# Eleven result tiles, stores behind the loads, and three smaller moves in a scheduled attention-and-MoE kernel

## The chip, the cores and the metric

One core of one Trainium2 chip. The metric is the device time of one execution in microseconds (us); where several runs are given, their median. Engines are named as in the profile: PE (matmul), DVE (VectorE), ACT (ScalarE), POOL (GpSimd), SP (which issues DMAs). Each engine works through its own instructions in order and waits on semaphores for the others.

## The reference

```
kv  = einsum('bhsd,bhse->bhde', k, v)        # 8 batches, 8 heads, 576 positions, 64 wide
out = einsum('bhsd,bhde->bhse', q, kv)
out = out / sqrt(mean(out*out, -1) + 1e-6) * g_norm
x   = out, heads side by side, as [4608, 512]

h   = x @ w_in                               # [4608, 1024]
e   = exp(h - max(h));  sm = e / (sum(e) + 1e-9)
u   = h * sm
ln  = (u - mean(u)) / sqrt(var(u) + 1e-6) * g_ln
y   = ln @ w_out                             # [4608, 512]
```

The kernel takes exp(h) without the maximum and doesn't divide by the sum: u = h e^h, and the missing factor goes into the variance's small constant. The mean and g_ln are folded into w_out ahead of time (w_mean, w_center), so that the last matmul's rows only need one factor each, rstd.

## The kernel before

**Tiling.** The 4608 tokens are nine chunks of 512. Chunks 0 to 7 are eight ninths of the batches 0 to 7; chunk 8 is the last ninth of all of them (q_last, collected by the pieces ql0 to ql7). Head pairs share 128 partitions.

**Pieces.** Nothing is looped in the order that it runs. Each piece of work has a name, is registered with `plan.add` (its engine, what it needs, the tiles it takes and uses) and is called in the order of one text, ORDER (lines 68 to 121). That text was written by a planner; the kernel only reads it. A token like `b1.0/dve@ob4` is: piece b of chunk 1, part 0, on DVE, its result in the slot ob4. Slots are single buffers: L (9 KB a partition; k and v of a batch, u, squares), M (4.6 KB; q, e, x), ob (results), osq, lss, rst (small ones) in SBUF, and P (two banks) and S (one bank) in PSUM. A slot is reused as soon as its last user is done; semaphores for that are set by the framework from the order. SLOTS (line 19) gives the counts for the planner.

**One chunk** runs through these pieces:

- k, v, q: loads, cast to bf16 by GpSimd's DMA queue (line 269; "a" and "b" are halves in batches 0 and 1). wi and wo load the weights.
- kv: k^T v of a batch on PE, 4 head pairs, into a P slot; kc.0, kc.1, kc.2: three copies out of it into kvd (line 319). Part 0 is the matrix as it lies, parts 1 and 2 are its two halves with the partitions turned over, for heads whose q lies in the other half.
- qt, qc: q turned by PE and copied out (chunks 0 to 4); qx: q turned by a DMA on SP (chunks 5 to 8).
- o: q times kv on PE; sq, s, ln, ex (ScalarE and PE; the mean square over a head by a matmul, then its root); x on DVE scales o into the input of the MoE part. Chunks 6 to 8 have rows instead of features up: o, sq, vd, vl, vg, x, xt, where vg is a product on GpSimd and xt a DMA transpose on SP.
- h: x times w_in on PE; e: exp on ScalarE; u: h times e on DVE; r: squares of u, for the variance. For chunks 0 to 2 (features up) r is a full tile of squares, g adds up pairs of e on GpSimd, z sums u, r and g over the features by matmuls, y and st turn that into the variance. For chunks 3 to 8 (rows up) e, u and r give their sums by the way (accum_out), st joins the three (row_stats, line 710) and t turns u by a DMA on SP.
- rs: the root of the variance on ScalarE; a: u times w_out on PE into a P or S slot; b: its rows scaled by rstd, on DVE or ScalarE, into an ob slot; d: the store, from SP's, GpSimd's or (chunk 8) ScalarE's queue. Chunk 8's last part goes in two halves of columns, a8.3|0 and a8.3|1.

**The gate.** `gate` (line 341) is a small copy on GpSimd that reads the last q loaded, q7, and stands ahead of the first DMA transpose, t3.0: no transpose starts before the loads are done. warm0 to warm8 are matmuls on zeros between the first pieces.

**Lines of the steps below.** 206 warm, 269 loads, 314 kv, 173 and 175 copies (kc, qc, ql, casts), 343 gate, 359 qt, 407 and 470 o, 420 sq, 435 s, 439 ln, 443 ex, 453 x, 495 vg, 572 and 581 h, 592 and 599 e, 607 and 612 u, 622 and 624 r of chunks 0 to 2 (ScalarE, GpSimd), 630 and 632 r of chunks 3 to 8 (ScalarE, DVE), 637 t, 643 g, 691 z, 714 to 720 row statistics, 767 and 774 a, 782 and 784 b, 799 and 801 d.

Of the kernel before, what the change touches and what calls it, by code (L numbers as in the profile page):

```python
# [857 lines left out]
```

## Time and profile before

| | |
|---|---|
| median of 3 runs | 182.4 us (181.66 to 182.57) |
| profiled execution | 181.77 us, span 179.7 us |
| granted PE clock | 0.999 |
| read from memory, written | 32.54 MB, 9.44 MB |

The profile shows one execution. A row of the timeline gives start, length (us), engine, line, operation, result and operands, how often, and in brackets the idle time ahead of it and what ended that. A row of groups gives line, engine, operation, shapes and count, then busy time and mean length (ns), then the idle time ahead and who ended it. A row of DMA issues gives the queue, the count, the size of each and the median time to landing. The table of windows gives, for each stretch, its length, the busy time (and instructions) of PE, weight loads, DVE, ACT and POOL, the granted clock, the DMA engines' mean share and GB/s. The chain of waits gives start, length and what the end was waiting for.

### The profile page before, as it was taken

Reading aid. Unit: us, or ns where it says so; the run is one execution under the profiler, and the core shown is the slowest. Engines: PE = TensorE matmul, PEld = TensorE weight load, DVE = VectorE, ACT = ScalarE, POOL = GpSimd, SP = SyncE. Lnnn points to the kernel's source line nnn. Section 1 sums busy time; section 2 is a strip of 40 time slices with the busy share of each in tenths; the row PEclk is TensorE's granted clock in tenths of the full one; section 3 lists DMA queues with packets and bytes.
Section 4 is the critical chain, followed back from the end, with each engine's and each line's share of the span. In section 5 each row is a group of like instructions: output and inputs, shape, how many; then the busy total and the mean of one; then the engine's idle time right before and its main releaser. Section 6 shows DMA issues by size and latency. Waiting matters only on the chain.

```text
span 179.7 us, 4520 instructions
## 1 busy us (share of the span) xinstructions
PE 164.9 (92%) x1808; PEld 81.1 (45%) x1831; DVE 127.1 (71%) x222; ACT 128.1 (71%) x239; POOL 71.9 (40%) x83
## 2 busy tenths in 40 slices
PE   6899958699999999999998999899999999999990
PEld 3344435345435565454443444444445444444450
DVE  2327599258874776667998869999788987948630
ACT  2377794593899687979879898469979746986210
POOL 7941596040899998100140006501132960222000
PEclk9999999999999999999999999999999999999999
DMA  5999999999999999999799999999998689968994
GB/s 170 252 207 275 353 208 209 205 208 222 248 233 232 209 207 198 277 214 206 157 172 203 206 216 220 152 256 245 171 227 239 99 166 248 200 139 215 175 256 125
DMA packets 60424, 37.81 MB, mean 210 GB/s; under 512 B 42140, under 2 KB 55204, under 8 KB 60404
## 3 DMA queue, kind: packets, MB, share of 16 engines
q0 software_dynamic: 15456, 20.16, 58.1%
q1 hardware_dynamic: 44036, 15.87, 44.1%
q10 hardware_dynamic: 912, 1.51, 3.1%
q8 instruction: 14, 0.23, 0.5%
q14 instruction: 6, 0.05, 0.1%
HBM read 32.54 MB, written 9.44 MB: 234 GB/s over the span
## 4 chain that ended last, share of the span: by engine, by line
PE 63%; DMA 22%; DVE 6%; issue 3%; POOL 1%; SPq 1%; ACT 1%; POOLq 0%; DVEq 0%; ACTq 0%
PE ps_S L767 20%; PE ps_P L581 19%; DMA sb_M<-in_q_dram 9%; PE ps_P L572 8%; PE ps_P L767 5%; DMA out_dram<-sb_ob 4%; DMA sb_L<-in_v_dram 4%; DMA sb_M<-sb_M 3%; PE ps_S L359 2%; DVE sb_ob L784 2%; PE ps_P L314 2%; PE ps_P L407 2%; DMA sb_L<-sb_L 2%; PE ps_P L691 1%; PE ps_S L435 1%
## 5 line engine op out<-in xcount | busy, mean ns | idle before, releaser
L767 PE MATMUL ps_S<-w_out_sb,sb_L 128*128 128x512 bf16 x220 | 53.1, 379 | 2.9 <-issue 2.4
L581 PE MATMUL ps_P<-w_in_sb,sb_M 128*128 128x512 bf16 x188 | 42.7, 379 | 1.0 <-ACT kvd L173 0.8
L767 PEld LDWEIGHTS <-sb_L 128*128 128x128 bf16 x280 | 26.4, 98 | 33.4 <-issue 3.3
L612 DVE SCALAR_TENSOR_TENSOR sb_L<-ps_P,sb_M 128x1024 bf16<-128x1024 f32 x24 | 29.1, 1222 | 8.4 <-ACT sb_M L599 8.2
L599 ACT ACTIVATE sb_M<-ps_P 128x1024 f32<-128x1024 f32 x24 | 24.5, 1023 | 8.2 <-PE ps_P L581 7.1
L581 PEld LDWEIGHTS <-sb_M 128*128 128x128 bf16 x192 | 18.7, 98 | 23.3 <-issue 0.9
L495 POOL TENSOR_TENSOR sb_M<-rr,g_rep 128x1024 f32<-128x1024 f32 x6 | 12.3, 2061 | 30.4 <-ACT rr L491 23.7
L572 PE MATMUL ps_P<-sb_M,w_in_sb 128*128 128x512 bf16 x94 | 21.9, 379 | 0.1
L607 DVE TENSOR_TENSOR sb_L<-ps_P,sb_M 128x1024 bf16<-128x1024 f32 x12 | 14.6, 1222 | 8.2 <-ACT sb_M L592 8.2
L453 DVE SCALAR_TENSOR_TENSOR sb_M<-ps_P,g_cols,sb_rst 128x512 bf16<-128x512 f32 x24 | 18.0, 790 | 2.9 <-ACT sb_rst L443 2.6
L784 DVE TENSOR_SCALAR sb_ob<-ps_S,rstd 128x512 f32<-128x512 f32 (+1 forms) x19 | 13.8, 735 | 7.7 <-PE ps_S L767 2.2
L592 ACT ACTIVATE sb_M<-ps_P 128x1024 f32<-128x1024 f32 x12 | 12.2, 1024 | 6.9 <-PE ps_P L572 6.9
L643 POOL TENSOR_TENSOR sb_M<-sb_M 128x512 bf16<-128x512 f32 x12 | 15.1, 1278 | 4.9 <-ACT sb_M L592 4.8
L420 ACT ACTIVATE sb_osq<-ps_P 128x512 bf16<-128x512 f32 x24 | 13.4, 596 | 4.6 <-PE ps_P L407 4.6
L630 ACT ACTIVATE sb_M<-sb_L 128x1024 bf16<-128x1024 bf16 x14 | 14.6, 1047 | 0.0
L572 PEld LDWEIGHTS <-w_in_sb 128*128 128x128 bf16 x96 | 9.2, 98 | 10.5 <-issue 0.2
L801 POOL DMA_DIRECT2D out_dram<-sb_ob x10 | 6.3, 633 | 16.4 <-DVE sb_ob L784 8.8
L632 DVE SCALAR_TENSOR_TENSOR sb_M<-sb_L 128x1024 bf16<-128x1024 bf16 x10 | 12.8, 1276 | 0.1
L443 ACT ACTIVATE sb_rst<-sb_lss 128x512 f32<-128x512 f32 x20 | 12.0, 632 | 0.1
L767 PE MATMUL ps_P<-w_out_sb,sb_L 128*128 128x512 bf16 x47 | 11.4, 379 | 0.1
L206 PE MATMUL ps_S<-zeros 128*128 128x512 bf16 (+1 forms) x18 | 8.5, 591 | 1.8 <-DVE zeros L188 1.5
L624 POOL TENSOR_TENSOR sb_L<-sb_L 128x1024 bf16<-128x1024 bf16 x4 | 7.6, 1910 | 6.1 <-DVE sb_L L607 6.0
(96 smaller groups left out, 211.2 us busy)
## 6 DMA issues: line engine op xcount, KB each, us to landing
out_dram<-sb_ob SPq DMA_DIRECT2D x14, 256.0 KB, 4.2
sb_L<-in_k_dram POOLq DMA_DIRECT2D x6, 576.0 KB, 12.2
sb_L<-in_v_dram POOLq DMA_DIRECT2D x6, 576.0 KB, 13.1
sb_M<-in_q_dram POOLq DMA_DIRECT2D x6, 576.0 KB, 12.3
out_dram<-sb_ob POOLq DMA_DIRECT2D x10, 256.0 KB, 4.8
sb_L<-in_moe_w_out_dram POOLq DMA_DIRECT2D x2, 1024.0 KB, 15.8
out_dram<-sb_ob SPq DMA_DIRECT2D x10, 128.0 KB, 3.0
sb_M<-in_q_dram POOLq DMA_DIRECT2D x4, 288.0 KB, 7.0
```

What stands on the lines that cost most here:

```text
L420: nc.scalar.activation(out=t[:, :], in_=T["o", c, hf][:, z], func=AF.Square)
L453: nc.vector.scalar_tensor_tensor(out=T["x", c][:, pairs_of(c, hf), :, z], in0=T["o", c, hf][:, z].rearrange("p (n q) -> p n q", n=2), scal ...
L572: nc.tensor.matmul(t[:, f % 2], w_in_sb[:, dt, f * 128:(f + 1) * 128], T["x", c][:, dt].rearrange("p q z -> p (q z)"), start=(dt == 0), st ...
L581: nc.tensor.matmul(T["h", c, m][:, half], x_block(c, m, dt), w_in_sb[:, dt, half * 512:half * 512 + 512], start=(dt == 0), stop=(dt == NP ...
L599: nc.scalar.activation(out=t.rearrange("p a b -> p (a b)"), in_=T["h", c, m].rearrange("p a b -> p (a b)"), func=AF.Exp, accum_out=T["zsum ...
L607: nc.vector.tensor_tensor(out=flat(T["u", c][:, 2 * p:2 * p + 2, :]), in0=flat(T["h", c, p]), in1=flat(T["e", c, p]), op=MUL)
L612: nc.vector.scalar_tensor_tensor(out=T["un", c][:, m, :], in0=T["h", c, m].rearrange("p a b -> p (a b)"), scalar=1.0, in1=T["e", c, m].rea ...
L630: nc.scalar.activation(out=unused, in_=src, func=AF.Square, accum_out=by)
L632: nc.vector.scalar_tensor_tensor(out=unused, in0=src, scalar=1.0, in1=src, op0=MUL, op1=MUL, accum_out=by)
L643: nc.gpsimd.tensor_tensor(out=T["es", c][:, n, :], in0=e[:, 0, :], in1=e[:, 1, :], op=ADD)
L767: nc.tensor.matmul(T["acc", c, m][:, 0], T["u", c][:, f, m * 128:(m + 1) * 128], w_out_sb[:, f, :], start=(f == 0), stop=(f == NF - 1))
L784: nc.vector.tensor_scalar_mul(out=t[:, :], in0=src, scalar1=T["rstd", c][:, m:m + 1])
```

## The change

Five things at once.

1. **Slots.** SLOTS names 11 ob slots (7 before) and 9 L slots (8 before). The old table uses ob0 to ob5 and L0 to L6; the new one ob0 to ob10 and L0 to L6.
2. **Stores.** In the old table the eight stores of chunks 0 and 1 (d0.0 to d1.3) stand ahead of the gate, among the loads; in the new one the first store, d0.0, comes behind the gate.
3. **kvd** becomes three tiles, one for each part, and kv_of picks the tile of its half.
4. **Squares and statistics.** r of chunks 3 to 8 may be on ScalarE alone (before 14 there and 10 on DVE; now 24). r of chunks 0 to 2: 4 on ScalarE and 8 on GpSimd (before 8 and 4). The row statistics of chunks 3 to 8 move from four operations on DVE to six on GpSimd, with two constant tiles. ql may no longer be on DVE.
5. **The table** is new throughout.

```diff
-SLOTS = {"P": 3, "S": 2, "L": 8, "M": 13, "osq": 4, "lss": 3, "rst": 4, "ob": 7}
+SLOTS = {"P": 3, "S": 2, "L": 9, "M": 13, "osq": 4, "lss": 3, "rst": 4, "ob": 11}
...
-    kvd = big.tile([128, B, 2, 2, 2, D], BF16, name="kvd")
+    kvd = [big.tile([128, B, 2, 2, D], BF16, name=f"kvd{i}") for i in range(3)]
...
+    per_u = big.tile([128, 4], FP32, name="per_u")
+    nc.vector.memset(per_u, -1.0 / d_ff)
+    per_z = big.tile([128, 4], FP32, name="per_z")
+    nc.vector.memset(per_z, 1e-6 * d_ff)
...
-        dst = kvd[:, b]
+        dst = kvd[part][:, b, ms].rearrange("p m x d -> p x m d")
         if part == 0:
-            copy(engine, dst[:, 0, :, ms, :], src)
+            copy(engine, dst, src)
         else:
             r = part - 1
-            copy(engine, dst[64 * r:64 * r + 64, 1, :, ms, :], src[64 - 64 * r:128 - 64 * r])
-
-    def kv_of(b, n, swapped):
-        return kvd[:, b, swapped ^ (n % 2), n % 2, n // 2, :]
+            copy(engine, dst[64 * r:64 * r + 64], src[64 - 64 * r:128 - 64 * r])
+
+    def kv_of(b, n, swapped, half):
+        return kvd[1 + half if swapped ^ (n % 2) else 0][64 * half:64 * half + 64, b, n // 2, n % 2, :]
...
-        plan.add(f"ql{b}", ("pool", "dve", "act"), lambda e, b=b: take_last(b, e), [f"q{b}{g}" for g in halves(b)], uses=[("q", b)])
+        plan.add(f"ql{b}", ("pool", "act"), lambda e, b=b: take_last(b, e), [f"q{b}{g}" for g in halves(b)], uses=[("q", b)])
...
-                plan.add(f"r{c}.{m}", ("act", "dve"), lambda e, c=c, m=m: row_usq(c, m, e), [f"u{c}.{m}"],
+                plan.add(f"r{c}.{m}", ("act", "act"), lambda e, c=c, m=m: row_usq(c, m, e), [f"u{c}.{m}"],
...
-        nc.vector.scalar_tensor_tensor(out=a[:, :], in0=us, scalar=-1.0 / d_ff, in1=us, op0=MUL, op1=MUL)
...
+    def row_stats(c):
+
+        def product(name, in0, in1, op):
+            t = small.tile([128, 4], FP32, name=name)
+            nc.gpsimd.tensor_tensor(out=t[:, :], in0=in0[:, :], in1=in1[:, :], op=op)
+            return t
+
+        a = product("a", T["usum", c], T["usum", c], MUL)
+        a = product("a2", a, per_u, MUL)
+        d = product("d", T["zsum", c], T["zsum", c], MUL)
+        d = product("d2", d, per_z, MUL)
+        f = product("f", a, T["qsum", c], ADD)
+        T["vare", c] = product("vare", f, d, ADD)
...
-            plan.add(f"st{c}", "dve", lambda c=c: row_stats(c), [f"{n}{c}.{m}" for n in "eur" for m in range(4)])
+            plan.add(f"st{c}", "pool", lambda c=c: row_stats(c), [f"{n}{c}.{m}" for n in "eur" for m in range(4)])
```

Of the tables, the places that the prediction speaks of. The start, from the middle of chunk 0 on (old, then new):

```
h0.0+@P0 wo0@L2 h0.1+ h0.2+@P1 h0.3+ h0.0 h0.1 h0.2 wo1@L3 table e0.0@M3 u0.0@L1 h0.4+@P2 k1a@L0 h0.5+ v1a h0.3 h0.4
e0.1@M4 h0.5 e0.2@M5 h0.6+@P0 h0.7+ q1a@M6 k1b v1b g0.0@M7 g0.1 g0.2 r0.0/act@L4 h0.6 h0.7 e0.3@M1 g0.3 wm0@S1 u0.1
r0.1/act u0.2 u0.3 r0.2/act r0.3/act wm1 wc4 kv1a@P2 kc1a.1/act kc1a.0/act warm6@S0 qt1.0@S0 z0@P0 warm7@P1
kc1a.2/act wc1 wc2 qc1.0/act@M1 o1.0@P2 warm8@S0 wc3 sq1.00@osq0 sq1.01@osq1 kv1b@P1 kc1b.1/act kc1b.2/act wc5 wc0
```
```
ex0.10@rst0 x0.10 ex0.11@rst1 table k1b v1b h0.2+@P0 h0.3+ x0.11 h0.0 h0.1 h0.2 e0.0@M4 h0.3 h0.4+@P2 h0.4
u0.0@L1 q1b k2@L4 e0.1@M5 u0.1 h0.5+ h0.5 e0.2@M6 u0.2 wm0@S1 wm1 wc2 r0.0/act@L5 wc3 wc4 wc5 h0.6+@P0 h0.6 wc1
h0.7+ h0.7 g0.0@M7 g0.1 e0.3@M1 kv1a@P2 kc1a.0/dve r0.1/pool kc1a.1/act warm6@S0 v2 qt1.0@S0 qc1.0/dve@M3 kc1a.2/act
q2@M5 k3@L6 warm7@P1 v3 q3@M4 o1.0@P2 g0.2 sq1.00@osq1 wc0 sq1.01@osq0 warm8@S0 kv1b@P1 r0.2/pool s1.00@S0 u0.3
...
ln1.11@lss0 ex1.10@rst0 ex1.11@rst1 a0.11 x1.10 x1.11 r0.3/pool g0.3 z0@S1 y0 st0 h1.0+@P2 h1.1+ rs0 b0.0/dve@ob0
```

Chunks 3 and 4, and the gate, in the new table:

```
a1.30@S1 s3.10@P0 ex3.00@rst0 ex3.01@rst2 g2.2 sq3.11@osq1 b1.2/dve@ob6 ln3.10@lss1 a1.31 s3.11@S0 ex3.10@rst1
ln3.11@lss2 qt4.1@P0 x3.00@M3 x3.01 r2.2/pool r2.3/pool b1.3/dve@ob7 qc4.1/dve o4.0@P1 sq4.00@osq1 ex3.11@rst2
o4.1@P0 sq4.01@osq0 s4.00@S0 ln4.00@lss2 ex4.00@rst0 sq4.10@osq1 x3.10 x3.11 g2.3 z2@S1 y2 st2 s4.01@S0 ln4.01@lss2
h3.00@P2 v7 x4.00@M1 h3.01 ex4.01@rst2 x4.01 s4.10@S0 e3.0@M2 u3.0@L6 a2.00@S1 q7@M9 a2.01 ln4.10@lss2 sq4.11@osq1
kv5@P1 kc5.0/dve kc5.2/dve rs2 ex4.10@rst2 s4.11@S0 ln4.11@lss1 r3.0/act kc5.1/dve gate@L2 t3.0 qx5@M2 h3.10@P2
ex4.11@rst0 x4.10 x4.11 h3.11 e3.1@M5 h3.20@P1 h3.21 e3.2@M4 u3.1 u3.2 h3.30@P0 h3.31 e3.3@M3 h4.00@P2 h4.01
h4.10@P1 t3.1 h4.11 u3.3 r3.1/act d0.0/sp e4.0@M7 u4.0@L5 e4.1@M5 u4.1 kv6@P0 kc6.1/act ql6/pool kc6.2/act gb
```

The end (old, then new):

```
b7.2/act@ob2 a7.31 d7.1/sp a8.00@S0 a8.01 a8.10@S1 a8.11 t8.2 u8.3 r8.3/dve t8.3 a8.20@P2 a8.21 b7.3/dve@ob4 d7.2/sp
d7.3/sp st8 rs8 b8.0/dve@ob5 d8.0/act a8.3|0@S0 a8.3|1@P0 b8.1/dve@ob0 d8.1/act b8.2/act@ob3 b8.3|0/dve@ob1 d8.2/act
b8.3|1/dve@ob2 d8.3|0/act d8.3|1/sp
```
```
a8.00@S1 a8.01 r8.1/act r8.2/act r8.3/act st8 b7.2/dve@ob2 a8.10@S0 a8.11 a8.20@P0 t8.3 rs8 b7.3/act@ob0
b8.0/act@ob5 d7.1/pool b8.1/act@ob6 d7.2/sp d7.3/pool d8.0/act a8.21 b8.2/act@ob4 d8.1/act d8.2/act a8.3|0@S0
b8.3|0/dve@ob10 d8.3|0/act a8.3|1@S1 b8.3|1/dve@ob2 d8.3|1/sp
```

106 lines of the change are left out of this document (40 added, 66 removed).

## The prediction

> **What bounds the kernel now.** First the page, then stages, then the engines' waits.
>
> ```profile
> span 179.7 us, 4520 instructions
> PE 164.9 (92%) x1808; PEld 81.1 (45%) x1831; DVE 127.1 (71%) x222; ACT 128.1 (71%) x239; POOL 71.9 (40%) x83
> ```
> ```profile
> 15.50:40.00 24.50, 20.52 (x257) 10.72 (x259) 15.28 (x25) 18.14 (x31) 11.94 (x14) 1.00 1.22 246
> 40.00:60.00 20.00, 19.49 (x255) 9.66 (x257) 14.01 (x18) 16.16 (x27) 14.59 (x13) 1.00 1.19 231
> 60.00:80.00 20.00, 19.48 (x409) 11.08 (x412) 14.95 (x29) 15.50 (x28) 12.07 (x13) 1.00 1.19 222
> 80.00:100.00 20.00, 19.42 (x102) 8.63 (x103) 16.74 (x31) 17.57 (x35) 2.81 (x4) 1.00 1.01 188
> 100.00:120.00 20.00, 19.03 (x290) 9.18 (x291) 17.86 (x30) 14.68 (x30) 5.03 (x4) 1.00 1.09 211
> 120.00:140.00 20.00, 19.64 (x210) 9.72 (x212) 16.83 (x28) 17.26 (x36) 5.04 (x5) 1.00 1.05 213
> 140.00:160.00 20.00, 19.89 (x93) 9.01 (x94) 16.91 (x31) 15.03 (x32) 8.25 (x9) 1.00 0.88 177
> 160.00:170.00 10.00, 9.95 (x47) 4.57 (x47) 6.55 (x15) 5.58 (x13) 1.55 (x3) 1.00 0.87 183
> ```
>
> Columns of the stages: length, then busy time of PE, weight loads, DVE, ACT, POOL, the clock, the DMA share and GB/s. PE's work (the same matmuls in both kernels) sets the end. Between 15.5 and 170 us PE idles 7.1 us, 4.0 of them before 40 us and never more than 1.0 in a later stage. That is all a reordering can win there; at the two ends stand loads and the last stores. The DMA share, about 1.2 until 80 us, is its ceiling here: the loads fill the DMA engines from the start, at 207 GB/s written where nothing else runs:
>
> ```profile
> 82.50:85.00 2.50, 2.50 (x20) 0.97 (x18) 1.88 (x4) 2.50 (x6) 0.00 (x0) 1.00 1.21 207
> 87.50:90.00 2.50, 2.45 (x13) 1.14 (x12) 2.45 (x5) 1.96 (x5) 0.87 (x3) 1.00 0.26 79
> 45.00:47.50 2.50, 2.50 (x24) 1.17 (x23) 2.18 (x3) 2.16 (x4) 2.12 (x2) 1.00 1.15 280
> 88.83 0.18 POOL L343 COPY sb_L<-sb_M 1x1 bf16<-1x1 bf16 x1 [13.32 <-DMA sb_M<-in_q_dram]
> 97.81 0.41 PE L407 MATMUL ps_P<-sb_M,kvd 64*64 64x256 bf16 x8 [0.37 <-DMA sb_M<-sb_M]
> ```
>
> The last load lands at 88.8 us (the gate's copy waited for it); behind it come the turned tiles, and o5.0, PE's first user of one, waits only 0.37 us. So the loads' end is nearly off PE's path.
>
> **The start: GpSimd's queue grows.** Up to q1a nothing gets earlier: the loads have the same order, and PE waits for q1a in both.
>
> ```profile
> 6.68 1.64 POOL L277 DMA_DIRECT2D sb_L<-in_moe_w_out_dram x2
> 9.40 0.72 POOL L269 DMA_DIRECT2D sb_L<-in_v_dram  x1 [0.38 <-DMA sb_L<-in_k_dram]
> 14.75 0.72 POOL L269 DMA_DIRECT2D sb_L<-in_v_dram  x1 [1.82 <-DMA w_in_sb<-in_moe_w_in_dram]
> sb_L<-in_k_dram POOLq DMA_DIRECT2D x6, 576.0 KB, 12.2
> sb_L<-in_moe_w_out_dram POOLq DMA_DIRECT2D x2, 1024.0 KB, 15.8
> sb_L<-in_v_dram POOLq DMA_DIRECT2D x3, 288.0 KB, 15.7
> L643 POOL TENSOR_TENSOR sb_M<-sb_M 128x512 bf16<-128x512 f32 x12 | 15.1, 1278 | 4.9 <-ACT sb_M L592 4.8
> L624 POOL TENSOR_TENSOR sb_L<-sb_L 128x1024 bf16<-128x1024 bf16 x4 | 7.6, 1910 | 6.1 <-DVE sb_L L607 6.0
> 27.57 0.62 PE L359 MATMUL ps_S<-ident,sb_M 128*128 128x128 bf16 x8 [0.30 <-DMA sb_M<-in_q_dram]
> 28.19 1.23 PE ps_P L691 x80
> 38.51 1.03 PE L572 MATMUL ps_P<-sb_M,w_in_sb 128*128 128x512 bf16 x4
> ```
>
> GpSimd's tenth load (v1a, 9.40) waited for its second (k0b) to land, its thirteenth (14.75) for its fifth (wi0): eight are outstanding at most. The new table puts the fifteenth, k2, ahead of g0.0; it waits for the seventh, wo0, which lands at 6.7 + 15.8 = 22.5. Until then g0.0 stands behind it, where it started at 19.5 before. From there GpSimd has k2 0.75, g0.0 and g0.1 2.56, r0.1 1.91, five loads 3.75, g0.2 1.28, r0.2 and r0.3 3.82, g0.3 1.28: 14.6 us, to 37.9. Those three squares were ScalarE's. z0 needs g0.3. PE, starting at 27.6 with qt1.0, has 7.5 us ahead of z0 and about 1 us of waiting for the second halves of v1 and q1: it is there at 36.1 and waits. z0 takes 1.23, so h1.0+ comes at 39.1; before it came at 38.5. **+0.6 us**; bounds 0 (GpSimd's fixed part runs faster) and +1.9 (one more square's length late).
> The same crossing returns at z1, which moves up past h2 in PE's order: r1.2 on GpSimd should end just when PE arrives. 0, at most +1.9.
>
> **Stores out of the loads.** d0.0 to d1.3, eight stores of 256 KB, leave the loads' time. In the stretch from 45.0 us, 280 x 2.5 = 700 KB moved; without one 262 KB store, 438 KB of loads need 2.12 us at 207 GB/s, so a store costs 0.4 us. Upper bound: from the end of v1b's load (14.75 + 15.7 = 30.5) to 88.8 are 58.3 us; less 18.5 loads of 590 KB (576 KB in the row) at 207 GB/s, 52.7, that leaves 5.6, over eight: 0.7. The last load lands 3 to 6 us earlier, at 83 to 86. The wait at 97.81 goes (−0.4). What is late next is PE's own order. The eight stores return behind the gate, into the same number of free microseconds. The four additional result tiles make room for them; on SP, d0.0 and d0.1 stand ahead of qx6, whose user o6.0 comes 8 us of PE's work later. The ninth large buffer does not exist: both tables name L0 to L6 only, and no function reads SLOTS. Price 0.
>
> **k^T v in three tiles.** One wait of this kind reached PE:
>
> ```profile
> 114.48 0.41 DVE L175 CAST kvd<-ps_P 128x256 bf16<-128x256 f32 x1
> 114.93 0.74 ACT L173 CAST kvd<-ps_P 64x256 bf16<-64x256 f32 x2 [3.00 <-DVE kvd L175]
> 115.72 8.79 PE L581 MATMUL ps_P<-w_in_sb,sb_M 128*128 128x512 bf16 x40 [0.75 <-ACT kvd L173]
> ```
>
> kc7.1 on ScalarE waits for kc7.0 on DVE, though they write different places of the one tile; PE's next user of that bank waits 0.75. With own tiles the wait goes: **−0.75**. The copies' sizes stay.
>
> **Squares and statistics.**
>
> ```profile
> L630 ACT ACTIVATE sb_M<-sb_L 128x1024 bf16<-128x1024 bf16 x14 | 14.6, 1047 | 0.0
> L632 DVE SCALAR_TENSOR_TENSOR sb_M<-sb_L 128x1024 bf16<-128x1024 bf16 x10 | 12.8, 1276 | 0.1
> L718 DVE TENSOR_TENSOR f<-a,qsum 128x4 f32<-128x4 f32 x6 | 1.0, 163 | 1.7 <-ACT sb_M L630 1.6
> L453 DVE SCALAR_TENSOR_TENSOR sb_M<-ps_P,g_cols,sb_rst 128x512 bf16<-128x512 f32 x24 | 18.0, 790 | 2.9 <-ACT sb_rst L443 2.6
> L420 ACT ACTIVATE sb_osq<-ps_P 128x512 bf16<-128x512 f32 x24 | 13.4, 596 | 4.6 <-PE ps_P L407 4.6
> L443 ACT ACTIVATE sb_rst<-sb_lss 128x512 f32<-128x512 f32 x20 | 12.0, 632 | 0.1
> masks.py:199 POOL TENSOR_SCALAR_AFFINE_SELECT eye<-eye 9x9 f32<-9x9 f32 x1 | 0.2, 192 | 0.1
> ```
>
> DVE loses ten squares, 12.8 us, and the statistics (six chunks of four operations near 0.16, 4 us). ScalarE gains 10 x 1.05 and gives four squares of chunks 0 to 2 to GpSimd: +6 net, +10 behind 85 us, where it was busy 73 to 88% of the stages up to 160 us. Its work in order is then the tight one. The worst place lies earlier: from ex3.00 to ex4.11 the new table gives ScalarE eight L443, six logarithms of like length, five L420, e3.0, r3.0 and rs2, about 14 us, beside 10.2 us of PE work (a1.31 to h3.11), because chunks 3 and 4 are normed together. PE meets it twice. o4.1 needs the bank that qc4.1 copies out, and qc4.1 stands on DVE behind x3.00 and x3.01 (L453) and b1.3, 2.3 us that wait for the late ex3.00: 0.9 us. h3.00 needs x3.11 behind ex3.11, which now stands behind sq4.00: 0.3. With half a microsecond for small waits elsewhere up to 100 us that is 1.7. Before, the three stages from 40 to 100 us idled 1.6. Net **0**, bounds −0.6 and +3. Behind 100 us the −0.4 and −0.75 stand against queueing on ScalarE; I take one more wait as long as the kvd one, +0.75: net **−0.4**, bounds −1.1 and +2.5.
> Row statistics: six operations on GpSimd, nearest rows 0.10 (a 9x9 memset) to 0.19, so 0.6 to 1.2 us against 0.55; they stand behind r.3 and ahead of rstd, and behind GpSimd's stores and vg products. Chunks 3 to 7 have a spare ob or bank; chunk 8 is in the tail.
> The Trainium skill (GPSIMD Engine Reference, 4.1 Engine selection) speaks against this move: it puts two-input elementwise work at about twice VectorE's time. By it the six would take 6 x 0.33 = 2.0 us, an estimate, and the tail 0.8 us more; no run here shows it yet.
>
> **The tail.**
>
> ```profile
> 170.53 2.81 ACTq L799 DMA_DIRECT2D out_dram<-sb_ob  x4
> 173.60 0.69 ACT L782 ACTIVATE sb_ob<-ps_P,rstd 128x512 f32<-128x512 f32 x1 [3.95 <-DMA out_dram<-sb_ob]
> 173.82 1.04 PE L774 MATMUL ps_P<-w_out_sb,sb_L 128*128 128x256 bf16 x8
> 174.32 2.46 ACTq L799 DMA_DIRECT2D out_dram<-sb_ob  x4
> ```
>
> ScalarE issued four stores behind b8.2 and ended at 176.8; the span ends 2.9 later, in landing. The new order has r8.1 to r8.3, rs8, b7.3, b8.0, b8.1, d8.0, then b8.2 and six issues. b8.2 no longer waits for its tile (3.95). a8.3|1 starts at 173.8, a8.3|0 0.9 before it, so a8.2 is there at 172.9; b8.2 ends at 173.8 behind a cross-engine step, and six issues of 0.61 end at 177.5: **+0.7**, bounds 0 and +1.5.
>
> **The sum.** +0.6 + 0 + 0 − 0.4 + 0.7 = +0.9 us. The profiled execution took 181.77 (span 179.7 and 2.07 around it), so 182.7 for one like it; the median of the runs, 182.4, lies 0.6 above it and gives **183.3**. A measurement here can't tell less than about 0.5%, 0.9 us, from no change.
>
> **Rivals.**
> A. The forecast, a small loss from GpSimd's late z0 and ScalarE's longer tail: 182.5 to 184.5, chance 0.42.
> B. The earlier gate and the split tiles win: z0 is on time (0), −1.1 behind 90 us, the crowd at chunks 3 and 4 costs 0.6 less, the tail 0: −1.7, 180.7. For it: the rows at 97.81 and 115.72, and DVE's 17 us. Against: PE's idle stages are already under 1.0. Decides if h1.0+ starts by 38.5. Chance 0.28.
> C. ScalarE becomes the bound: the 14 us against 10.2 reach PE almost whole (+3) and the squares behind 100 us cost 2.5: with 0.6 and 0.7 from start and tail less the 1.1, +5.7, 188.1; taken at half, between those ends, 185.3. For it: in-order queue, 88% in the stage from 80 us. Against: PE has kv5, a2.0 and h3 to do meanwhile. Chance 0.22.
> D. The deferred stores collide with the transposes: 3 to 6 us more of DMA where the share was 1.0 to 1.1; xt6.1 late by 2 us at h6.20, on top of A: 185.3. Against: the gate opens as much earlier. Chance 0.08.
> A's lower part counts as same: faster 0.27, same 0.28, slower 0.45. Range 180.2 to 187.5; A alone 182.5 to 184.5.
>
> **What would show it.** z0 starting at 37 to 39 behind GpSimd's g0.3; the gate's copy at 83 to 86; no PE wait for kvd copies; ScalarE ending its last stores near 177.5 with a span near 180.6. Wrong, if PE idles over 2 us in any stage behind 40 us (C or D), or if h1.0+ starts before 38 us.

## The result and the profile after

| | before | after |
|---|---|---|
| median of the runs beside each other | 182.49 us (181.66 to 182.80) | 187.64 us (186.93 to 189.72) |
| profiled execution | 181.77 us, span 179.7 us | 186.93 us, span 185.1 us |
| granted PE clock | 0.999 | 0.988 |

The ratio is 1.0308, interval 1.0214 to 1.0403: slower by about 5 us, just above the range of 180.2 to 187.5 and well off the 183.3 that was forecast. Some executions of most kernels run 1 to 3% longer: the medians here and below are of all executions, the ratios leave those slow ones out, and two profiles are of slow ones, that with three stores put off and that with the split tile alone. In the rows below, code that stood at line L in the kernel before stands some five lines further down (L407, o, is L412; L637, t, is L642). First the head of the page of the changed kernel, then its stages in the columns of before.

```profile
span 185.1 us, 4536 instructions
...
PE 169.1 (91%) x1831; PEld 82.1 (44%) x1831; DVE 111.5 (60%) x178; ACT 134.9 (73%) x255; POOL 88.3 (48%) x132
```
```profile
80.00:100.00 20.00, 16.07 (x262) 7.98 (x247) 10.40 (x20) 14.11 (x28) 3.67 (x10) 0.91 1.05 184
100.00:120.00 20.00, 20.00 (x124) 9.13 (x123) 15.30 (x22) 18.22 (x37) 6.19 (x13) 1.00 1.03 208
120.00:140.00 20.00, 20.00 (x243) 9.84 (x241) 14.19 (x19) 16.97 (x37) 7.72 (x13) 1.00 0.85 145
140.00:160.00 20.00, 19.84 (x98) 8.88 (x93) 12.75 (x17) 15.74 (x32) 7.70 (x16) 1.00 0.96 216
160.00:170.00 10.00, 8.94 (x41) 3.87 (x40) 4.16 (x7) 6.70 (x16) 4.44 (x9) 1.00 0.89 212
```

The reader is to see two holes and a slack clock: PE idles 3.93 us from 80 to 100 us, where before it idled 0.58, at a mean clock of 0.91 in place of 1.00, and 1.06 us from 160 to 170, where before it idled 0.05. Between them, in the stages in which ScalarE was feared as the bound, PE idles 0.16 us in 60. Next PE's own order around both holes.

```profile
89.94 1.90 PE L772 MATMUL ps_S<-w_out_sb,sb_L 128*128 128x512 bf16 x8
95.78 0.64 PE L412 MATMUL ps_P<-sb_M,kvd 64*64 64x256 bf16 x8 [3.94 <-DMA sb_M<-sb_M]
...
97.73 1.55 PE L772 MATMUL ps_S<-w_out_sb,sb_L 128*128 128x512 bf16 x4
...
99.34 1.03 PE L772 MATMUL ps_S<-w_out_sb,sb_L 128*128 128x512 bf16 x4
...
161.88 1.02 PE L772 MATMUL ps_S<-w_out_sb,sb_L 128*128 128x512 bf16 x4 [0.67 <-DVE sb_ob L789]
...
165.16 1.89 PE L586 MATMUL ps_P<-w_in_sb,sb_M 128*128 128x512 bf16 x8 [0.39 <-DVE sb_L L617]
```

**The first loss** is o5.0, the first user of a tile turned by DMA: 3.94 us for qx5, and behind the gap the same four matmuls take 1.55 us that take 1.03 at 99.34. Who issued what at that time: SP's queue, then GpSimd's.

```profile
85.64 5.33 SPq L375 DMA_TRANSPOSE sb_M<-sb_M  x1
91.01 1.31 SPq L642 DMA_TRANSPOSE sb_L<-sb_L  x1
92.37 1.31 SPq L806 DMA_DIRECT2D out_dram<-sb_ob  x2
93.79 4.18 SPq L375 DMA_TRANSPOSE sb_M<-sb_M  x1
```
```profile
83.94 0.18 POOL L348 COPY sb_L<-sb_M 1x1 bf16<-1x1 bf16 x1 [9.10 <-DMA sb_M<-in_q_dram]
...
85.02 1.87 POOL L806 DMA_DIRECT2D out_dram<-sb_ob  x3
```

In the chain of waits qx5 stands from its issue to its landing, first in the kernel before, then in the changed one:

```profile
92.04 5.72 DMA sb_M<-sb_M
```
```profile
85.64 10.09 DMA sb_M<-sb_M
```

Put side by side (a landing is taken as the end of the wait for it):

| us | before | after | earlier by |
|---|---|---|---|
| the gate's copy | 88.83 | 83.94 | 4.9 |
| qx5 issued by SP | 92.04 | 85.64 | 6.4 |
| qx5 landed | 97.77 | 95.73 | 2.0 |
| PE has nothing ahead of o5.0 (start less wait) | 97.44 | 91.84 | 5.6 |

The loads did end early, as forecast. The new table lets PE reach o5.0 5.6 us earlier; but the transpose, which took 5.73 us from issue to landing, now takes 10.09, with three stores of 256 KB issued on GpSimd from just before its issue on (85.02 to 86.89). **The second loss** is the pair of waits at 162 and 165 us; the experiments take it apart.

### The profile page after: what moved, and what is told of

It reads as the page before. It is cut to its first block, busy times and chain, and to the rows that moved or that the text cites. A ratio compares the mean times of both kernels' runs of the same rounds, so it can differ in the third digit from the quotient of the medians.

```text
span 185.1 us, 4536 instructions
## 1 busy us (share of the span) xinstructions
PE 169.1 (91%) x1831; PEld 82.1 (44%) x1831; DVE 111.5 (60%) x178; ACT 134.9 (73%) x255; POOL 88.3 (48%) x132
## 4 chain that ended last, share of the span: by engine, by line
PE 61%; DMA 22%; issue 5%; DVE 4%; SPq 2%; ACT 2%; POOL 2%; DVEq 0%; POOLq 0%; ACTq 0%
PE ps_S L772 20%; PE ps_P L586 17%; DMA sb_L<-in_v_dram 8%; PE ps_P L577 8%; DMA sb_M<-sb_M 5%; DMA w_in_sb<-in_moe_w_in_dram 5%; PE ps_P L772 5%; DMA out_dram<-sb_ob 3%; PE ps_P L319 2%; PE ps_S L440 2%; PE ps_S L696 2%; PE ps_P L412 2%; PE ps_S L364 1%; ACT sb_M L604 1%; SPq L642 1%
## 5 line engine op out<-in xcount | busy, mean ns | idle before, releaser
L772 PE MATMUL ps_S<-w_out_sb,sb_L 128*128 128x512 bf16 x224 | 53.0, 382 | 0.7 <-DVE sb_ob L789 0.7
L586 PE MATMUL ps_P<-w_in_sb,sb_M 128*128 128x512 bf16 x192 | 43.9, 379 | 0.5 <-DVE sb_L L617 0.4
L772 PEld LDWEIGHTS <-sb_L 128*128 128x128 bf16 x280 | 27.0, 98 | 33.1 <-issue 2.3
L635 ACT ACTIVATE sb_M<-sb_L 128x1024 bf16<-128x1024 bf16 x24 | 25.0, 1045 | 0.0
L500 POOL TENSOR_TENSOR sb_M<-rr,g_rep 128x1024 f32<-128x1024 f32 x6 | 11.4, 1900 | 12.7 <-ACT rr L496 9.4
L719 POOL TENSOR_TENSOR f<-a,qsum 128x4 f32<-128x4 f32 x6 | 1.2, 200 | 32.4 <-ACT sb_M L635 32.4
L629 POOL TENSOR_TENSOR sb_L<-sb_L 128x1024 bf16<-128x1024 bf16 x8 | 15.1, 1893 | 0.0
L772 PE MATMUL ps_P<-w_out_sb,sb_L 128*128 128x512 bf16 x56 | 13.6, 379 | 0.0
L175 DVE CAST kvd<-ps_P 64x256 bf16<-64x256 f32 (+3 forms) x13 | 4.8, 371 | 13.1 <-PE ps_P L319 9.6
L787 ACT ACTIVATE sb_ob<-ps_S,rstd 128x512 f32<-128x512 f32 x11 | 7.5, 688 | 5.8 <-PE ps_S L772 5.0
```

Source lines behind the costliest of these rows:

```text
L586: nc.tensor.matmul(T["h", c, m][:, half], x_block(c, m, dt), w_in_sb[:, dt, half * 512:half * 512 + 512], start=(dt == 0), stop=(dt == NP ...
L629: nc.gpsimd.tensor_tensor(out=dst, in0=src, in1=src, op=MUL)
L635: nc.scalar.activation(out=unused, in_=src, func=AF.Square, accum_out=by)
L772: nc.tensor.matmul(T["acc", c, m][:, 0], T["u", c][:, f, m * 128:(m + 1) * 128], w_out_sb[:, f, :], start=(f == 0), stop=(f == NF - 1))
```

## The experiments

Fifteen kernels were run, each beside the kernel before on the same chip. Theory 1: stores behind the gate slow the transposes, and PE meets that at the first user of one. Theory 2: with the stores late, results meet tiles that have not been stored. The rivals: ScalarE's longer queue, or the row statistics on GpSimd.

### Three stores wait for qx5

```diff
+    def gate2():
+        t = small.tile([1, 1], BF16, name="gate2")
+        nc.gpsimd.tensor_copy(t[:, :], T["qT", 5][0:1, 0, 0:1])
+    plan.add("gate2", "pool", gate2, ["qx5"], uses=[("qT", 5)])
...
-d0.1/sp d0.2/pool o5.0@P2 b2.0/act@ob2
+d0.1/sp gate2 d0.2/pool o5.0@P2 b2.0/act@ob9
```

> The changed kernel, but GpSimd's three stores d0.2, d0.3 and d1.0, which were issued at 85 to 87 us beside the transpose qx5, wait until qx5 has landed (a one-element copy ahead of them on GpSimd; b2.0 gets another result tile). Theory 1 (these stores share the DMA engines with qx5 and take its landing from about 6 us to 10.1): qx5 lands 5.5 to 7 us behind its issue, near 91.5 to 92.5, PE's wait at o5.0 falls from 3.9 to under 1 us, the granted clock stays at 1.00 in the stage from 80 to 100 us, time 182.5 to 184 instead of 187.6. Rival (qx5 is slow by itself, as the first long transpose behind the loads): it lands 9 to 10 us behind its issue as before, PE waits 3.5 to 4 us, time 187 to 188. Rival 2 (PE would only wait elsewhere): the wait goes and the time falls by less than 2 us.

Measured: 185.62 us (184.63 to 186.55), ratio 1.0174 [1.0124, 1.0224]. SP's queue, ScalarE and PE of this run:

```profile
85.61 3.21 SPq L379 DMA_TRANSPOSE sb_M<-sb_M  x1
...
92.04 6.57 SPq L379 DMA_TRANSPOSE sb_M<-sb_M  x1
```
```profile
102.23 1.02 ACT L608 ACTIVATE sb_M<-ps_P 128x1024 f32<-128x1024 f32 x1 [4.42 <-DMA sb_M<-sb_M]
```
```profile
91.60 0.41 PE L416 MATMUL ps_P<-sb_M,kvd 64*64 64x256 bf16 x8 [0.27 <-DMA sb_M<-sb_M]
103.88 3.34 PE L776 MATMUL ps_S<-w_out_sb,sb_L 128*128 128x512 bf16 x8 [3.11 <-ACT sb_lss L448]
```

Freed of the three stores, qx5 is issued in 3.21 us where it took 5.33, and o5.0's wait of 3.94 shrinks to 0.27. The stores now meet the next transpose, qx6, whose issue grows to 6.57 us. Its user o6.0 comes late enough; but e4.2 writes the large tile that qx6 still reads, so ScalarE waits 4.42 us, and PE 3.11 behind it. The stall moved with the stores. So theory 1 had the landing and the wait right and the time wrong: it is 1.6 us above the range expected and nearly what rival 2 allowed.

### e4.2 in a tile of its own

On top of the run before:

```diff
-"M": 13
+"M": 14
...
-x5.01 e4.2@M0
+x5.01 e4.2@M13
```

> The changed kernel with the gate for d0.2, d0.3, d1.0 behind the landing of the transpose qx5 (as in the run that gave 185.6 us), and besides e4.2 in a large tile of its own, so that ScalarE no longer waits for the late transpose qx6 to have read that tile. Theory 1 (the deferred stores slow whichever transpose they meet, and the loss reaches PE only through the user of that transpose): the wait of 4.4 us of ScalarE and of 3.1 us of PE near 102 to 104 us goes, the clock stays at 1.00 there, and the time is 182.3 to 183.6 us. Rival (the transposes are not the cause; ScalarE's queue is, and PE would meet it elsewhere): 185 us or more, with another wait of 2 to 3 us for ScalarE between 100 and 115 us.

Measured: 184.61 us (183.48 to 187.01), ratio 1.0128 [1.0069, 1.0187]. Both waits of that run are gone and the clock is 1.00 in every stage; the time is 1 us above the expected range. What is left are three waits of PE behind 120 us, 1.3 us for a result on ScalarE, 1.3 for an x of DVE and 1.0 for a turned tile. So the second loss has grown; that it is for tiles whose stores come late is tried below.

### The stores put off in the kernel before: three, then five

Nothing else is changed; the results that wait longer get tiles of their own. The diff is that with five; with three, d1.1 and d1.2 stay where they were and there are ten tiles.

```diff
-"ob": 7
+"ob": 12
...
-d0.2/sp d0.3/sp
...
-d1.0/sp
...
-d1.1/sp d1.2/sp
...
-gate@L3
+gate@L3 d0.2/pool d0.3/pool d1.0/pool d1.1/pool d1.2/pool
```

> The kernel before, with three stores of 256 KB (d0.2, d0.3, d1.0) taken from SP among the loads and issued on GpSimd's queue right behind the gate, with three more result tiles to hold them; nothing else. Theory 1 (stores behind the gate slow the transposes by more than the loads gain): the gate 1 to 2 us earlier, near 87; qx5 takes 8 to 10 us from issue to landing in place of 5.7, o5.0 waits 2 to 4 us, and the time is 183.5 to 186 us. Rival (stores cost the same few tenths anywhere, as the prediction had it): the gate earlier, o5.0's wait 0 to 0.4, and 181.5 to 182.4 us.

> The kernel before with five stores (d0.2, d0.3, d1.0, d1.1, d1.2) behind the gate on GpSimd's queue in place of three. Theory 1: the wait at o5.0 grows with the number of stores: 2.5 us with three, 3.5 to 5 with five, with 1 to 1.3 us more for the clock that falls behind the gap; 185.2 to 187.5 us. Rival (the transpose only shares the DMA engines with the first stores, so more of them change nothing): 184 to 185 us, with 2.5 us of wait as with three.

Measured: three, 184.51 us (182.14 to 185.64), ratio 1.0105 [1.0070, 1.0140]; five, 184.47 us (182.98 to 188.13), ratio 1.0091 [1.0038, 1.0144]. In the run with five, on GpSimd, SP and PE:

```profile
85.56 0.18 POOL L342 COPY sb_L<-sb_M 1x1 bf16<-1x1 bf16 x1 [10.51 <-PE ps_S L434]
86.06 3.13 POOL L800 DMA_DIRECT2D out_dram<-sb_ob  x5 [0.32 <-issue]
```
```profile
89.54 10.69 SPq L369 DMA_TRANSPOSE sb_M<-sb_M  x2
```
```profile
99.40 0.64 PE L406 MATMUL ps_P<-sb_M,kvd 64*64 64x256 bf16 x8 [2.51 <-DMA sb_M<-sb_M]
```

This is the larger part of the change's second point (five of its eight stores), alone, and it alone makes the kernel 0.9% slower. The five stores gave the loads 3.3 us (85.56 against 88.83), 0.65 each, inside the prediction's upper bound of 0.7. SP issued qx5 2.5 us earlier and it landed 1.6 us later, at 99.36: 9.8 us in place of 5.7. That the wait would grow with the number of stores was a miss: it is 2.5 us with three and with five, and the time lies in the rival's range (184 to 185). Of the 4.1 us by which the landing grew with five, 2.5 are hidden because the transpose was issued that much earlier; the other 1.6, the 0.5 us by which PE came earlier in this run and the 0.4 that it waited before make the wait. The queues between 86 and 100 us, five stores first, then the kernel before (packets, MB, share of the 16 engines' time):

```profile
q1 hardware_dynamic: 5527, 1.39, 66.0%
q0 software_dynamic: 512, 1.61, 37.4%
```
```profile
q1 hardware_dynamic: 6522, 1.65, 64.6%
q0 software_dynamic: 455, 0.84, 27.1%
```

Nearly all of q1 are transposes, in packets of some 250 bytes. q0 is GpSimd's queue, 3 KB a packet on average: nearly all of its 1.61 MB are the five stores and a sixth that stands there in both kernels. The shares add up to about the whole in both (103% and 92%), so it is likely that what the stores take is taken from the transposes. The Trainium skill (DMA: Bandwidth & Descriptors, Queues, rings and completion order) says that an engine takes turns between queues packet by packet; the longer landing agrees with that, though no run here sets the packet sizes against each other.

### Sixteen matmuls of zeros in the gap

```diff
-WARM = (4, 4, 3, 3, 2, 2, 2, 5, 1)
+WARM = (4, 4, 3, 3, 2, 2, 2, 5, 1, 16)
...
-d0.2/pool o5.0@P2 b2.0/act@ob2
+d0.2/pool b2.0/act@ob9 warm9@S1 o5.0@P2
```

> The changed kernel with sixteen matmuls of zeros (3.5 us at full clock) ahead of o5.0, in the gap in which PE waits for the turned tile qx5 (b2.0 is put ahead of them and takes another result tile, since they write its bank). Theory (the gap costs twice: 3.9 us of waiting, and 1.3 us more because the granted clock falls to 0.5 to 0.85 from 95 to 99 us): o5.0 starts at 95.5 to 96.3 as before, the clock stays at 1.00 behind it, and the time is 1 to 1.5 us less, 186.1 to 186.7 us. Rival (the clock falls with the work, not with the gap): 187.5 us or more.

Measured: 186.55 us (185.67 to 186.57), ratio 1.0222 [1.0188, 1.0257]. Stretches of two microseconds, first the changed kernel, then with the gap filled (the clock is the third number from the end):

```profile
92.00:94.00 2.00, 0.00 (x0) 0.00 (x0) 0.00 (x0) 0.83 (x2) 0.00 (x0) 1.00 1.22 197
94.00:96.00 2.00, 0.23 (x8) 0.19 (x12) 0.00 (x0) 0.00 (x0) 0.00 (x0) 0.85 1.25 212
96.00:98.00 2.00, 2.00 (x89) 1.45 (x82) 0.56 (x2) 1.23 (x3) 0.00 (x0) 0.50 1.15 323
98.00:100.00 2.00, 2.00 (x9) 0.80 (x8) 0.71 (x2) 1.40 (x3) 0.00 (x0) 0.80 1.71 267
```
```profile
94.00:96.00 2.00, 1.70 (x8) 0.59 (x6) 0.00 (x0) 0.00 (x0) 0.00 (x0) 1.00 1.19 169
96.00:98.00 2.00, 1.93 (x92) 1.38 (x93) 0.82 (x2) 1.47 (x4) 0.00 (x0) 1.00 1.21 347
98.00:100.00 2.00, 2.00 (x11) 0.89 (x10) 1.04 (x3) 1.77 (x4) 0.00 (x0) 1.00 1.21 270
```

(The DMA share of 1.71 at 98 us shows that the prediction's 1.2 is what the loads reach, and not a ceiling of the engines.) The transpose lands no earlier and o5.0 even starts 0.3 us later (96.07), but the clock stays at 1.00, and by the run of eight L772 matmuls that starts at 102.36 in the changed kernel and at 101.36 here, PE is 1.0 us ahead. So a gap of 3.9 us on PE costs about 5 in all there. The median is in the range expected, but between the profiled spans only 0.3 us are left (184.8 against 185.1): the second loss takes the rest back, 1.46 us of idle PE from 160 to 170 us where the changed kernel has 1.06.

### Result tiles and e8.0

e8.0 in another tile, alone, and then with the three stores behind qx5 and b6.0 in ob1:

```diff
-h8.01 t7.1 e8.0@M5
+h8.01 t7.1 e8.0@M0
```

> The changed kernel, but e8.0 writes a free tile (M0) in place of M5, which xt8.1 still reads. Theory 2 (ScalarE stands 1.7 us at e8.0 for the transpose xt8.1, so rs6, b6.0 and b6.1 come late and PE waits 0.67 us at a7.00 and 0.39 at h8.30): ScalarE's wait goes, both PE waits shrink, time 1 to 1.5 us below the changed kernel, about 186.2 to 186.7. Rival (the late end is set by the store tiles on SP's queue, behind t7.1 and t7.2): ScalarE waits at b6.0 for its ob tile in place, and the time is within 0.5 us of 187.6.

> Both edits, and b6.0 in a result tile that has long been stored (ob1). If the two waits add: 181 to 183, near the kernel before (182.4) or a little below. If the changed kernel loses elsewhere too: above 184.

Measured: alone 188.82 us (187.41 to 189.43), ratio 1.0339 [1.0282, 1.0396], no gain; with the stores behind qx5, 185.65 us (184.30 to 187.36), ratio 1.0137 [1.0079, 1.0195], no gain that can be told over the run with the stores behind qx5 alone. Both are misses; the second keeps the wait of 3.1 us near 103 us, and b6.1 still has its old tile in it. Then the tiles alone: fifteen, and every b takes the next of ob0 to ob14.

```diff
-"ob": 11
+"ob": 15
```

> The changed kernel with fifteen result tiles taken in turn, and nothing else. Theory (two losses, each with its own cause): the wait of 3.9 us at o5.0 and the slow clock behind it stay, the waits for result tiles behind 120 us go; 1.5 to 2.5 us less than the changed kernel, 185.2 to 186.3 us. Rival (the late stores behind 120 us are the first loss passed on, and tiles alone give nothing): 187 to 188 us.

Measured: 185.86 us (185.57 to 189.13), ratio 1.0191 [1.0158, 1.0224]. Why one cure alone did little is in these rows: DVE with e8.0 in another tile, then ScalarE and PE with fifteen result tiles.

```profile
161.26 0.75 DVE L788 TENSOR_SCALAR sb_ob<-ps_S,rstd 128x512 f32<-128x512 f32 x1 [4.73 <-DMA out_dram<-sb_ob]
```
```profile
155.66 1.02 ACT L603 ACTIVATE sb_M<-ps_P 128x1024 f32<-128x1024 f32 x1 [2.01 <-DMA sb_M<-sb_M]
```
```profile
161.06 1.02 PE L771 MATMUL ps_S<-w_out_sb,sb_L 128*128 128x512 bf16 x4 [0.95 <-DVE sb_ob L788]
```

Two waits lie on top of each other. With e8.0 freed, DVE stands 4.73 us before b6.1, whose tile holds a result of chunk 4 that SP stores only behind t7.1 and t7.2. With the tiles freed, ScalarE stands 2.01 us before e8.0, which writes a tile that xt8.1 still reads; r6, rs6 and the results of chunk 6 come behind it, and PE waits 0.95. Either one hides the other: PE's wait there, 0.67 us in the changed kernel, is 1.36 with e8.0 freed and 0.95 with the tiles freed. That the median fell by 1.8 us with fifteen tiles, as expected, is not their doing as far as the profiles show: the spans differ by 1.0 us, and 0.9 of it lies ahead of h1.0+ (at 37.67 us against 38.58), well before the first result that gets another tile. From h1.0+ to the end it is 146.4 us against 146.5.

### All of it

First only some tiles, on top of the run with e4.2 in its own tile, then in place of them fifteen in turn.

```diff
-e8.0@M5
+e8.0@M0
...
-b6.0/act@ob5 b6.1/dve@ob0 b6.2/act@ob2
+b6.0/act@ob1 b6.1/dve@ob7 b6.2/act@ob8
```

> The run before it, and near the end b6.0, b6.1, b6.2 in result tiles 1, 7 and 8, whose stores d2.2, d3.1, d3.3 have long landed, in place of 5, 0 and 2 (d4.2, d4.1, d4.0, which stand on SP behind the transposes t7.1 and t7.2), and e8.0 in tile M0. Theory 2 (the wait near 160 us is that for stores that came late on SP): DVE's wait of 5.0 us for a store at 160 us and the PE waits for results of DVE (2.3 us in the earlier run) go; 1 to 2 us less than the run before it, 181.0 to 182.5 us. Rival (PE waits there for ScalarE's squares and row sums): no gain over the run before it.

> The changed kernel with the gate for d0.2, d0.3, d1.0 behind qx5, e4.2 and e8.0 in tiles of their own (as in the run that gave 182.7 us), and fifteen result tiles taken in turn in place of eleven handed out by the table, so that a result meets the store of the fifteenth before it. Theory 2 in full (the waits of ScalarE for 3.1 us at 121 us and of DVE for 2.5 us at 143 us are for tiles whose stores came late): they go, with the PE waits of 1.7 and 1.0 us behind them; 1.5 to 2.7 us less, 180.0 to 181.5 us, ratio 0.985 to 0.995, which is faster than the kernel before. Rival (PE meets ScalarE's queue there anyway): 182.3 to 183, ratio 1.00.

Measured: 182.73 us (180.52 to 185.51), ratio 0.9986 [0.9947, 1.0024], a median just above its range; with fifteen tiles 180.45 us (179.31 to 182.35), ratio 0.9877 [0.9813, 0.9941]. The last is 1.2% faster than the kernel before. Its stages, and the waits of PE of over 0.2 us behind 88 us:

```profile
80.00:100.00 20.00, 19.61 (x240) 9.54 (x242) 13.57 (x23) 17.68 (x35) 3.87 (x11) 1.00 1.00 171
100.00:120.00 20.00, 19.84 (x212) 9.44 (x214) 15.90 (x23) 18.24 (x38) 8.61 (x16) 1.00 1.15 229
120.00:140.00 20.00, 19.89 (x151) 9.46 (x151) 14.81 (x19) 16.82 (x39) 7.70 (x12) 1.00 1.03 183
140.00:160.00 20.00, 19.89 (x93) 9.06 (x93) 11.59 (x16) 15.63 (x33) 8.73 (x22) 1.00 0.94 247
160.00:170.00 10.00, 9.69 (x45) 4.24 (x45) 2.70 (x6) 7.06 (x14) 4.30 (x12) 1.00 1.14 218
```
```profile
91.37 0.41 PE L416 MATMUL ps_P<-sb_M,kvd 64*64 64x256 bf16 x8 [0.23 <-DMA sb_M<-sb_M]
164.02 1.90 PE L776 MATMUL ps_P<-w_out_sb,sb_L 128*128 128x512 bf16 x8 [0.26 <-DVE sb_ob L793]
```

PE idles 1.1 us from 80 to 170 us (90 less 88.92), in the kernel before 2.1 (90 less 87.93). All 24 squares are on ScalarE here and the row statistics on GpSimd, so neither holds PE up under this table. Is the gain that of the tiles alone? The kernel before with the same fifteen:

> The kernel before with fifteen result tiles taken in turn in place of seven, and nothing else. Theory (before had no PE wait over 0.2 us for a result tile, so more of them win nothing): 181.8 to 182.5 us, ratio 1.00. Rival (the gain of the version with 180.4 us is that of the tiles alone): 180.3 to 181 us.

Measured: 181.50 us (180.99 to 183.79), ratio 0.9965 [0.9935, 0.9995]. So about 0.6 us of the 2.2 is to be had by tiles alone, a little more than the nothing that was expected; the rest belongs to the changed kernel. In the profiled executions the two kernels with fifteen tiles are 2.2 us apart (178.2 and 180.5), and 0.8 of that lies ahead of h1.0+ (37.89 against 38.73).

### k^T v: the split, and one engine

Two kernels, each the one before but for this: the tile split as in the change, then the tile whole and one copy on the other engine.

```diff
-    kvd = big.tile([128, B, 2, 2, 2, D], BF16, name="kvd")
+    kvd = [big.tile([128, B, 2, 2, D], BF16, name=f"kvd{i}") for i in range(3)]
```
```diff
-kv7@P0 kc7.0/dve kc7.1/act a4.10@S0 a4.11 st4 kc7.2/act
+kv7@P0 kc7.0/act kc7.1/act a4.10@S0 a4.11 st4 kc7.2/act
```

> The kernel before, with the tile of turned k^T v split in three, and nothing else. The prediction's price: -0.75 us (the wait of 0.75 at 115.7 us goes, as does ScalarE's wait of 3.0 for DVE): 181.6 us, ratio 0.996. Rival (a split tile changes which copy waits for which, and the wait only moves): 182.4, ratio 1.00.

> The kernel before with one copy, kc7.0, moved from DVE to ScalarE, so that the three copies out of that bank stand on one engine; the tile of k^T v stays whole. Theory 4 (engines that copy out of the same bank wait for one another, whatever tile they write): ScalarE's wait of 3.0 us for DVE at 112 to 115 us and PE's 0.75 go; 0.4 to 0.9 us less than before, ratio 0.995 to 0.998. Rival (PE's wait there is for the bank to be copied by whoever comes): ratio 1.00, PE waits 0.5 to 0.8 us as before.

Measured: the split alone 182.44 us (181.55 to 185.10), ratio 1.0015 [0.9982, 1.0049]; kc7.0 moved 181.49 us (181.06 to 184.44), ratio 0.9988 [0.9956, 1.0021]. ScalarE's copies with the split, then with one engine, and the stage of the latter:

```profile
117.58 0.74 ACT L173 CAST kvd<-ps_P 64x256 bf16<-64x256 f32 x2 [3.00 <-DVE kvd L175]
```
```profile
113.59 1.13 ACT L172 CAST kvd<-ps_P 128x256 bf16<-128x256 f32 x3 [1.19 <-PE ps_P L313]
```
```profile
100.00:120.00 20.00, 19.84 (x294) 9.76 (x296) 17.95 (x30) 15.58 (x31) 5.02 (x4) 1.00 1.12 211
```

With three tiles the wait is the same 3.00 us to the hundredth, and PE's 0.75 stands too. With one tile and one engine both are gone, and PE gains 0.81 us in the stage (19.84 against 19.03). What kc7.0 and kc7.1 have in common once they write different tiles is the P slot that both read, two banks. The changed kernel shows the other case: there kc4.1 on DVE runs from 59.33 to 59.75 us while ScalarE's copies out of another slot (kc3.2, kc3.0, kc3.1) run from 58.48 to 59.61; kc4.0 on ScalarE, out of kc4.1's slot and into another tile, then waits until 59.79. So the waiting goes by the slot; whether the chip or the order of the semaphores makes the copies wait, no run shows. The move's gain in time is too small for its interval.

### The code under the old table

The changed code with the table of before. The ten squares that stood on DVE are on ScalarE in the first kernel, and on DVE, as they were, in the second:

```diff
-r3.0/dve
+r3.0/act
...
-r3.2/dve
+r3.2/act
...
```

> All code parts of the change (three kvd tiles, squares of chunks 3 to 8 on ScalarE, row statistics on GpSimd, the constants) under the old table. If the parts cost little by themselves and the table did the harm: within 1.5 us of the kernel before, 181.5 to 184. If ScalarE's additional 10 us or GpSimd's statistics are the loss (rival C of the prediction): 185 to 189, with PE waiting for ScalarE in the stages behind 100 us.

> The changed code under the table of before, as in the run that gave 185.3 us, but with the ten squares of chunks 3 to 8 back on DVE where that table had them; the split of k^T v and the row statistics on GpSimd stay. Theory 3 (under a table that was not laid out for it, the ten squares make ScalarE late, and that was the 2.9 us): 182.2 to 183.2 us. Rival (the row statistics on GpSimd, behind its stores and products, are the cost): 184.5 us or more.

Measured: 185.29 us (185.23 to 188.28), ratio 1.0156 [1.0129, 1.0182]; with the squares on DVE 183.15 us (182.57 to 184.76), ratio 1.0059 [1.0019, 1.0098]. The ten squares cost 1.8 us (0.0097 of 182.4) under a table that was not laid out for them; the row statistics on GpSimd and the split together 1.1.

## Why the prediction was wrong

**The step that failed** is the one headed "Stores out of the loads". It said that the eight stores "return behind the gate, into the same number of free microseconds", price 0. They return into the landing of qx5, of which PE's order had no slack: 3.94 us of wait where 0.37 stood, and about 1.0 us of slow clock behind it. The gain in the loads was sized well: gate at 83.94 in the forecast 83 to 86. The mistake was to balance bytes against free time and not to follow them to the one transfer that PE needs next. The prediction even wrote "What is late next is PE's own order" and did not look where that order had moved o5.0: 5.6 us up. Shown by the stores behind qx5 and by the five stores in the kernel before. Its own sign of being wrong, PE idle over 2 us in a stage behind 40 us, came at 80 to 100 us, with 3.93.

**"The four additional result tiles make room for them"** failed too. With stores late on SP behind transposes, eleven tiles ran out behind 150 us. Together with the tile that e8.0 waits for, that is the second loss, 0.67 + 0.39 us of PE's waits. Neither cure alone takes it away; it is gone (0.26 us of waiting left) in the kernel that has both, in which the three stores also wait for qx5.

**The split of k^T v, −0.75:** the wait did go, but not for the reason given. The split alone wins nothing and leaves the wait. The new table puts the copies of kv7 on one engine (kc7.0 to kc7.2, all DVE), and one engine alone took the wait away in the kernel before.

**The start, +0.6:** the wait that was reckoned did not come. GpSimd's g0.3, then PE's last piece ahead of z0, z0, and h1.0+:

```profile
35.72 1.26 POOL L648 TENSOR_TENSOR sb_M<-sb_M 128x512 bf16<-128x512 f32 x1
```
```profile
36.39 1.02 PE L772 MATMUL ps_S<-w_out_sb,sb_L 128*128 128x512 bf16 x4
37.34 1.08 PE L696 MATMUL ps_S<-sb_L,stat_sel 128*32 128x128 bf16 x64
...
38.58 3.63 PE L577 MATMUL ps_P<-sb_M,w_in_sb 128*128 128x512 bf16 x16
```

g0.3 ends at 36.98, not 37.9, because k2 was issued at 21.76 rather than 22.5; and PE, reckoned at z0 by 36.1, came at 37.34, so z0 waited for nothing. (GpSimd's list adds up to 15.35 us, not 14.6; the 37.9 is worked out with the former.) h1.0+ is 0.07 us later than before, but PE had waited 0.93 us for a half of w_out at 24.14 in this execution. In seven of the nine profiles with this start h1.0+ comes at 37.6 to 37.9 us, 0.6 to 0.9 ahead of the 38.51 of before. So the start was a small gain as a rule, and not a loss. z1 met no wait, as forecast.

**The crowd at chunks 3 and 4, net 0:** o4.1 waited 0.5 us where 0.9 was reckoned and h3.00 not at all.

**ScalarE behind 100 us, +0.75:** 40.00 us of PE in 40 from 100 to 140 us, so nothing there. Rival C falls for this table; the ten squares on ScalarE cost 1.8 us only under the old one.

**The statistics:** six operations at 0.20 us each.

```profile
L719 POOL TENSOR_TENSOR f<-a,qsum 128x4 f32<-128x4 f32 x6 | 1.2, 200 | 32.4 <-ACT sb_M L635 32.4
```

That is the 1.2 us at the top of the forecast's 0.6 to 1.2. Against 163 ns for the same operation on DVE it is 1.2 times, not twice: the rule of the Trainium skill (GPSIMD Engine Reference, 4.1 Engine selection) that spoke against the move does not hold for a tile of 128x4.

**The tail, +0.7:** from PE's end to the span's end 5.1 us (180.0 to 185.1), before 4.8: +0.3.

**The rivals.** Rival D had the mechanism, deferred stores against transposes, with a chance of 0.08, but put it at xt6.1 and h6.20 and priced it at 2 us. It came at qx5, the first transpose behind the gate that feeds o, and cost over twice that. Its argument against, that "the gate opens as much earlier", is what the run with five stores measures: 3.3 us earlier, and still 2.5 us of wait. Rival B was right that z0 is on time; that its 180.7 us is nearly the 180.45 of the version in which both losses are taken out is luck, since that version has other tiles and stores than the kernel that B spoke of.

**The sum.** At three places PE has the same pieces behind it in both kernels: h1.0+, a6.30 and the end of its work. It comes to h1.0+ 0.07 us later than before, to a6.30 3.6 later (159.32 against 155.68), to its end 5.2 later (180.0 against 174.9), and the span ends 5.4 later. So 3.6 us are lost between the first two: 3.57 more of waiting for qx5 and about 1.0 of slow clock, less 0.75 at kv7 and, by difference, 0.25 that the table wins elsewhere. Another 1.5 are lost from a6.30 on, the second loss, of which the rows of PE's waits count 1.06, and 0.3 in the tail. Not settled: which of the changed kernel's parts gives the 1.6 us that the best version has over the kernel before with as many tiles; in the profiles 0.8 us lie in the start, and the rest is not assigned.

## What to carry to other kernels

When transfers are moved out of one stage, follow them to the first transfer of the next stage that the bounding engine waits for, and ask how much slack its user has in the new order; free DMA time on average says nothing about it. A table that brings the user forward by as much as the loads gain spends that gain before the transfer has shown that it can follow. Where a result buffer and an input buffer come late at the same place, curing one shows no gain: take both away before calling the theory wrong.

## What the runs showed of the hardware

A store of 256 KB cost about 0.65 us among the loads. Five of them, put off, lengthened the landing of one transpose from 5.7 to 9.8 us, with the DMA engines' mean share at 1.04 in the shorter landing and 1.15 in the longer.

Copies on two engines out of one P slot of PSUM ran one after the other, in program order, also where they wrote different tiles (a wait of 3.00 us for kc7.1), and copies out of two slots ran side by side (59.33 to 59.75 us beside 58.48 to 59.61). Whether the chip asks for this or the order of the semaphores alone, no run shows.

After a gap of 3.9 us on PE the granted clock was 0.85, 0.50 and 0.80 in the three stretches of two microseconds from 94 us on, and 1.00 throughout where zeros were multiplied in the gap. The Trainium skill (TensorE: Matmul & The Clock Gate, Part 1: The HAM clock gate) has the clock at half after an idle window of about 3.4 us and full again after as long a busy one. The trace agrees in the length of the fall: 0.15, 0.50 and 0.20 of two microseconds, over a half, are 3.4 us. It does not agree in how long a gap it takes: the clock fell to 0.50 behind a wait of 2.51 us in the run with five stores, and stayed at 1.00 behind one of 3.13 us in the run with e8.0 freed and the stores behind qx5.
